# Merged weight words in SBUF instead of PSUM, casts moved to VectorE, one chunk loaded later

## The chip, the cores and the metric

The kernel runs on one core of a Trainium2 chip. A core has TensorE (PE; its weight loads are listed as PEld), VectorE (DVE), ScalarE (ACT), GpSimd (POOL) and SyncE (SP, which only issues transfers and notes here). Each engine works through its own queue in order; semaphores join the queues. The metric is the device time of one launch in microseconds (us); lower is better.

## The reference, cut to what matters

```
w = softmax(weight_gen, axis=-1)               # (4, 4096, 8, 7): 7 taps for each of 8 heads
x_unf = 7 shifted copies of zero-padded x      # x: (4, 4096, 192), 24 channels per head
x2 = einsum('bshk,bskhg->bshg', w, x_unf)      # dynamic causal convolution
h = x2.reshape(16384, 192) @ w_in              # (192, 2048)
g = h            where h >= 1
    0            where h <= -1
    (h + 1)**2/4 elsewhere
out = g @ w_out                                # (2048, 192)
```

All is float32. TensorE multiplies in a shorter format, so the kernel splits every operand into a high and a low part and adds the products that matter.

## The kernel before, in words

The 16384 tokens are cut into 32 blocks of 512. For each block the convolution makes x, a transpose turns it, and it is split into hc (high) and hl (low). The 2048 hidden units are 16 groups of 128, worked on as 8 pairs; with 32 blocks that makes 256 pairs. A pair has a first product (`gemm1_pair`, 18 matmuls into two PSUM banks psh), a gate on ScalarE and VectorE (`relu`, `square`, `act_g`), a split of the gate into gh on ScalarE and gl on VectorE (`split_g`), and, two pairs later, a second product into the banks o (`gemm2_part`, two parts of 16 matmuls).

The weights are not ready when block 0 starts: they are decoded during it, in 8 chunks, chunk c being the w_in columns and w_out rows of pair c. Each chunk has two parts, w_in (part 0) and w_out (part 1). The steps for a chunk are:

- `load_weights(c)`: SyncE fetches the raw words into one of 4 buffers r.
- `cast_act` or `cast_dve`: the upper half of each word is turned into a half-precision head, on ScalarE or VectorE (line 327 or 331). One part is 384 elements wide.
- `merge(c, part)`: VectorE shifts the word and joins it with the head (line 340). It reads r and head, both in SBUF, and writes psw, a bank of the same four PSUM banks (pool `ps_h`) that the first product writes.
- `high(c, part)`: ScalarE copies psw into whi or wo, the high part (line 352).
- `low(c, part)`: VectorE subtracts the high part from psw and writes wlo or the second half of wo (line 356).

`early_pair(w)` handles the gate of pair w and decodes chunk w + 1 in one hand-written order, for w = 2 to 6. `first_pairs` does the same for pairs 0 and 1 with chunks 0 to 2, `edge_pair` ends block 0. Everything is emitted under a manual schedule: the order in the code is the order in each queue.

GpSimd meanwhile computes the convolution of block 1 (`conv`, lines 179 and 189: products of 1.55 us and adds of 1.85 us) in pieces that `wave(count)` takes from a list. Each piece waits for the newest entry of `marks`, that is the last merge or VectorE cast emitted before it. When the 13 pieces are done, ScalarE copies a strip (`again`), TensorE turns the result (`turn1`), and x of block 1 can be split; the first pair of block 1 needs that.

The second part of `gemm2_part` waits for a note: a no-operation on SyncE's queue, behind whatever transfers that queue has still to issue.

Of the kernel before, what the change touches and what calls it, by code (L numbers as in the profile page):

```python
# [10 lines left out]
F32 = mybir.dt.float32  # L11
F32R = mybir.dt.float32r
# [5 lines left out]
ALU = mybir.AluOpType  # L18
# [4 lines left out]
def kernel(  # L23
# [21 lines left out]
    nc = tc.nc  # L45
    P = 128
# [6 lines left out]
    NF = DFF // P  # L53
# [10 lines left out]
    N = n * P  # L64
# [15 lines left out]
    xt = ctx.enter_context(tc.tile_pool(name="xt", bufs=2))  # L80
    up = ctx.enter_context(tc.tile_pool(name="up", bufs=3))
    gp = ctx.enter_context(tc.tile_pool(name="gp", bufs=6))
    op = ctx.enter_context(tc.tile_pool(name="op", bufs=2))
    raw = ctx.enter_context(tc.tile_pool(name="raw", bufs=4))
    dram = ctx.enter_context(tc.tile_pool(name="dram", bufs=2, space=bass.MemoryType.DRAM))
    ps_h = ctx.enter_context(tc.tile_pool(name="ps_h", bufs=4, space=bass.MemoryType.PSUM))
# [129 lines left out]
    def conv_summed(b):  # L216

        g, gi = group_of[b]
        wt, xtile = w_t[g], x_t.pop(b)
        near = ps_o.tile([P, 2, 512], F32, tag="o1", name="near")  # L220
        wn = near[:, 0, 0:n * E].rearrange("p (j h k) -> p j h k", j=n, h=H)
        sums = ps_o.tile([P, 2, 512], F32, tag="o0", name="sums")
        acc = sums.rearrange("p a d -> p (a d)")[:, 0:n * D].rearrange("p (j h g) -> p j h g", j=n, h=H)
        nc.scalar.activation(out=wn, in_=wt[:, gi], func=AF.Copy)

        def times(eng, out, w, k):
            return eng.tensor_tensor(
                out=out, in0=xtile[:, k:k + n, :].rearrange("p j (h g) -> p j h g", h=H),
                in1=w[:, :, :, k:k + 1].to_broadcast([P, n, H, G]), op=ALU.mult)

        def alone(eng, w, k):
            t = whole()
            times(eng, by_head(t), w, k)
            again(t)
            return t

        def add(k):
            t = cv.tile([P, n, H, G], F32, tag="T", name="tap")
            times(nc.vector, t, wn, k)
            out = acc  # L240
            if k == KV - 1:
                own.append(whole())
                out = by_head(own[0])
            nc.vector.tensor_tensor(out=out, in0=acc, in1=t, op=ALU.add)

        own = []
        return alone, wn, wt[:, gi], lambda: times(nc.vector, acc, wn, 1), add, own
# [50 lines left out]
    C1 = NC * P  # L298
    CN = C1 + CF * D
    NCH = NF // CF  # L300
    UNIT = 2.0 ** 8
    raw_t, marks = {}, []

    def load_weights(c, behind=None):
        r = raw.tile([P, 4 * CN + 2], U16, tag="r", name="r")
        for h in range(2):
            f = c * CF + h
            load = nc.sync.dma_start(
                out=r[h * Q:(h + 1) * Q, 1:1 + 4 * C1].rearrange("q (k c) -> q k c", k=NC),
                in_=w_in[:, f * P:(f + 1) * P].rearrange("(k q) c -> q k c", q=Q).bitcast(U16))  # L310
            if behind is not None:
                tc.add_manual_dep(load.ins, behind.ins.name, SYNC, reason="the first block goes first")
                behind = None
        nc.sync.dma_start(
            out=r[:, 1 + 4 * C1:1 + 4 * CN].rearrange("p (f c) -> p f c", f=CF),
            in_=w_out[c * CF * P:(c + 1) * CF * P, :].rearrange("(f p) c -> p f c", p=P).bitcast(U16))
        raw_t[c] = r

    def tops(c, part):

        sl = (slice(0, C1), slice(C1, CN), slice(0, CN))[part]
        top = raw_t[c][:, 2:2 + 4 * CN].rearrange("p (c t) -> p c t", t=4)[:, sl, 2]
        return heads[c % 2][:, sl, 1].bitcast(F16), top.bitcast(BF16)

    def cast_act(c, part):
        o, i = tops(c, part)
        nc.scalar.activation(out=o, in_=i, func=AF.Copy, scale=0.5)

    def cast_dve(c, part):
        o, i = tops(c, part)  # L330
        marks.append(nc.vector.tensor_scalar(out=o, in0=i, scalar1=0.5, scalar2=None, op0=ALU.mult))  # L331

    psw = {}

    def merge(c, part):
        word = raw_t[c].bitcast(U32)[:, 1:1 + 2 * CN].rearrange("p (c t) -> p c t", t=2)[:, :, 0]
        upper = heads[c % 2].rearrange("p c t -> p (c t)").bitcast(U32)
        psw[c, part] = ps_h.tile([P, 512], F32, tag="h", name="psw")
        sl = (slice(0, C1), slice(C1, CN))[part]
        marks.append(nc.vector.scalar_tensor_tensor(  # L340
            out=psw[c, part].bitcast(U32)[:, 0:sl.stop - sl.start], in0=word[:, sl], scalar=13, in1=upper[:, sl],
            op0=ALU.logical_shift_right, op1=ALU.bitwise_or))
# [7 lines left out]
    def high(c, part):  # L350
        hi, lo, src = views(c, part)
        nc.scalar.activation(out=hi, in_=src, func=AF.Copy)  # L352

    def low(c, part):
        hi, lo, src = views(c, part)
        nc.vector.tensor_tensor(out=lo, in0=src, in1=hi.bitcast(F32), op=ALU.subtract)  # L356
        del psw[c, part]
# [27 lines left out]
    def relu(i):  # L385

        u = up.tile([P, 512], F32, tag="u", name="u")
        u_t[i] = u[:, 0:N]
        nc.scalar.activation(out=u_t[i], in_=h_t[i][:, 0:N], func=AF.Relu, scale=0.5 * UNIT, bias=0.5)  # L389

    def square(i):
        nc.scalar.activation(out=u_t[i], in_=u_t[i], func=AF.Square, scale=UNIT ** -0.5)  # L392

    def act_g(i):

        uv, pv = u_t.pop(i), h_t[i][:, 0:N]
        nc.vector.scalar_tensor_tensor(out=pv, in0=uv, scalar=1.0 / UNIT, in1=pv, op0=ALU.min, op1=ALU.max)  # L397

    def split_g(i):
        gv = h_t.pop(i)[:, 0:N]  # L400
        gh = gp.tile([P, 512], F32R, tag="gh", name="gh")
        gl = gp.tile([P, 512], F32R, tag="gl", name="gl")
        nc.scalar.activation(out=gh[:, 0:N], in_=gv, func=AF.Copy)  # L403
        nc.vector.tensor_tensor(out=gl[:, 0:N], in0=gv, in1=gh[:, 0:N].bitcast(F32), op=ALU.subtract)  # L404
        g_t[i] = (gh, gl)

    notes = []
# [89 lines left out]
    for b in range(2, NB):  # L497
        w = (b - 2) * NP
# [34 lines left out]
    with tc.manual_schedule():  # L533
# [19 lines left out]
        alone, near, far, second, add, own = conv_summed(0)  # L553
# [11 lines left out]
        for k, t in enumerate(pieces):  # L565
            for c in range(NC):
                turn_sum(src, t, k == 0, k == len(pieces) - 1, c)
        merge(0, 0)
        cast_dve(0, 1)
        high(0, 0)  # L570
        run(s1[4:6])
        low(0, 0)
        run(split_x(0, src, [nc.vector] * NC))
        cast_dve(1, 2)
        merge(1, 0)
        turned1 = whole()
        n_ops = conv(1, nc.gpsimd, marks, turned1)

        def wave(count):
            for _ in range(min(count, len(n_ops))):  # L580
                n_ops.pop(0)()
# [6 lines left out]

        def first_pairs():
            merge(0, 1)  # L590
            merge(1, 1)
            tc.add_manual_dep(s1[6]().ins, marks[-1].ins.name, SYNC, reason="the decoding of a chunk goes first")
            load_weights(4)
            load_weights(5)
            relu(0)
            high(1, 0)
            low(1, 0)
            gemm1_pair(1)
            cast_act(2, 0)
            high(0, 1)  # L600
            high(1, 1)
            low(0, 1)
            low(1, 1)
            cast_dve(2, 1)
            merge(2, 0)
            merge(2, 1)
            wave(3)
            load_weights(6)
            square(0)
            relu(1)  # L610
            high(2, 0)
            high(2, 1)
            square(1)
            act_g(0)
            low(2, 0)
            low(2, 1)
            act_g(1)
            split_g(0)
            relu(2)
            square(2)  # L620
            split_g(1)
            relu(3)
            square(3)
            act_g(2)
            act_g(3)
            split_g(2)
            split_g(3)
            cast_act(3, 0)
            cast_dve(3, 1)

        def early_pair(w):
            i, j, c = 2 * w, 2 * w + 1, w + 1
            merge(c, 0)
            merge(c, 1)
            wave(1)
            if c + 4 < NCH:
                load_weights(c + 4)
            relu(i)
            high(c, 0)
            high(c, 1)  # L640
            low(c, 0)
            low(c, 1)
            square(i)
            relu(j)
            square(j)
            act_g(i)
            if c + 1 < NCH:
                cast_dve(c + 1, 1)
            wave(1)
            act_g(j)  # L650
            split_g(i)
            split_g(j)
            if c + 1 < NCH:
                cast_act(c + 1, 0)

        def edge_pair(w):
            i, j = 2 * w, 2 * w + 1
# [18 lines left out]
        for w in range(NS // 2 + LAGP):  # L676
            i, j = 2 * w, 2 * w + 1
# [74 lines left out]
```

## Time and profile before

| | us |
|---|---|
| median of 3 runs | 1144.56 (1143.82 to 1144.73) |
| the profiled execution | 1144.88 |
| its span, first to last instruction | 1142.4 |
| TensorE busy | 1128.4 (99%) |
| ScalarE busy | 964.5 (84%) |
| VectorE busy | 834.3 (73%) |
| GpSimd busy | 792.4 (69%) |

Outside the span lie 2.5 us. TensorE's granted clock over the whole span is 0.997 of 2.4 GHz. Block 0 occupies the first 60 us; blocks 1 to 31 fill the rest.

### The profile page before, as it was taken

The numbers are of one execution on the slowest core, as the hardware profiler recorded it, in microseconds if no ns is written. First come the engines' busy times: TensorE is split into PE (matmuls) and PEld (weight loads), VectorE is DVE, ScalarE is ACT, GpSimd is POOL, SyncE is SP. The second block draws the span as 40 slices with busy tenths as digits, with TensorE's granted clock in tenths as the row PEclk, the third lists the DMA queues.
The fourth block names the chain that finished last, engine by engine and source line by source line (L and its number), as shares of the span: only waits on it lengthen the run. The fifth ranks groups of instructions, "written<-read, shape, count | busy, mean of one in ns | idle before, by whom it ended". The sixth has DMA issues, their size and how long they took to land.

```text
span 1142.4 us, 32241 instructions
## 1 busy us (share of the span) xinstructions
PE 1128.4 (99%) x12885; PEld 1112.8 (97%) x12885; DVE 834.3 (73%) x1271; ACT 964.5 (84%) x1745; POOL 792.4 (69%) x511
## 2 busy tenths in 40 slices
PE   7999999999999999999999999999999999999998
PEld 5889999999999999999999999999999999999998
DVE  8887867777676777767777677776767777677765
ACT  6878888888888888888888888888888888888886
POOL 4699876777857678486686866778576785866310
PEclk9899999999999999999999999999999999999999
DMA  9512222222222122222122222222222122221100
GB/s 230 116 67 83 92 85 92 72 64 79 90 78 91 59 74 89 73 96 90 44 90 73 86 91 78 65 73 90 77 92 72 61 91 82 81 91 43 48 24 29
DMA packets 84053, 91.43 MB, mean 80 GB/s; under 512 B 5056, under 2 KB 75712, under 8 KB 83904
## 3 DMA queue, kind: packets, MB, share of 16 engines
q1 hardware_dynamic: 83904, 89.39, 24.6%
q8 instruction: 101, 1.65, 0.6%
q14 instruction: 48, 0.39, 0.1%
HBM read 64.99 MB, written 24.38 MB: 78 GB/s over the span
## 4 chain that ended last, share of the span: by engine, by line
PE 96%; ACT 1%; DVE 1%; DMA 0%; POOL 0%; issue 0%; SPq 0%; DVEq 0%; POOLq 0%
PE psh L378 49%; PE o L432 46%; PE psx L267 1%; DMA x<-in_x_dram 0%; ACT u L392 0%; ACT u L389 0%; ACT gh L403 0%; DVE psh L397 0%; DVE psw L340 0%; ACT whi L352 0%; POOL piece L189 0%; POOL acc L189 0%; ACT wo L352 0%; DVE gl L404 0%; DVE wo L356 0%
## 5 line engine op out<-in xcount | busy, mean ns | idle before, releaser
L432 PE MATMUL o<-wo,gh 64*128 64x384 f32 x4096 | 638.3, 353 | 1.0 <-SPq L441 1.0
L432 PE MATMUL o<-wo,gl 64*128 64x192 f32 x4096 | 615.1, 247 | 0.0
L432 PEld LDWEIGHTS o<-wo,gh 64*128 64x128 f32 x4096 | 609.3, 184 | 2.4 <-SPq L441 1.2
L432 PEld LDWEIGHTS o<-wo,gl 64*128 64x128 f32 x4096 | 591.3, 188 | 0.7
L397 DVE SCALAR_TENSOR_TENSOR psh<-u,psh 128x512 f32<-128x512 f32 x512 | 354.4, 695 | 282.2 <-ACT u L392 281.8
L378 PE MATMUL psh<-hc,whi 64*128 64x512 f32 x1536 | 436.6, 396 | 3.6 <-DVE wlo L356 2.5
L378 PE MATMUL psh<-hc,wlo 64*128 64x512 f32 x1536 | 430.5, 389 | 0.0
L378 PE MATMUL psh<-hl,whi 64*128 64x512 f32 x1536 | 429.5, 388 | 0.0
L389 ACT ACTIVATE u<-psh 128x512 f32<-128x512 f32 x512 | 301.4, 589 | 79.0 <-PE psh L378 77.8
L404 DVE TENSOR_TENSOR gl<-psh,gh 128x512 fp32r<-128x512 f32 x512 | 345.2, 684 | 15.5 <-ACT gh L403 1.1
L403 ACT ACTIVATE gh<-psh 128x512 fp32r<-128x512 f32 x512 | 299.0, 591 | 64.7 <-DVE psh L397 64.7
L189 POOL TENSOR_TENSOR acc<-acc,pr 128x768 f32<-128x768 f32 x185 | 343.4, 1856 | 6.5 <-DVE head L331 2.8
L392 ACT ACTIVATE u<-u 128x512 f32<-128x512 f32 x512 | 324.3, 633 | 16.0
L179 POOL TENSOR_TENSOR pr<-x,w 128x768 f32<-128x768 f32 x186 | 286.6, 1548 | 7.0 <-DVE psw L340 7.0
L378 PEld LDWEIGHTS psh<-hc,whi 64*128 64x128 f32 x1536 | 270.6, 185 | 8.7 <-DVE wlo L356 3.9
L378 PEld LDWEIGHTS psh<-hl,whi 64*128 64x128 f32 x1536 | 270.5, 185 | 3.1 <-DVE hl L259 0.3
L378 PEld LDWEIGHTS psh<-hc,wlo 64*128 64x128 f32 x1536 | 270.9, 186 | 1.6
L259 POOL TENSOR_TENSOR hl<-XT,hc 128x512 fp32r<-128x512 f32 x90 | 115.8, 1303 | 206.9 <-PE o L432 151.6
L179 POOL TENSOR_TENSOR acc<-x,w 128x768 f32<-128x768 f32 x31 | 47.9, 1546 | 70.2 <-DVE w L155 68.3
L258 ACT ACTIVATE hc<-XT 128x512 fp32r<-128x512 f32 x90 | 55.5, 618 | 0.0
L284 DVE STREAM_TRANSPOSE T<-acc 128x768 f32<-128x768 f32 x30 | 50.2, 1672 | 0.0
L457 DVE SCALAR_TENSOR_TENSOR osb<-o,osb 128x384 f32<-128x384 f32 x64 | 32.5, 548 | 2.8 <-ACT osb L456 2.8
(44 smaller groups left out, 188.8 us busy)
## 6 DMA issues: line engine op xcount, KB each, us to landing
x<-in_x_dram SPq DMA_DIRECT2D x28, 960.0 KB, 5.0
XT<-D SPq DMA_DIRECT2D x180, 128.0 KB, 2.7
out_dram<-osb SPq DMA_DIRECT2D x31, 384.0 KB, 3.1
D<-T SPq DMA_DIRECT2D x30, 384.0 KB, 2.3
x<-in_x_dram SPq DMA_DIRECT2D x4, 945.0 KB
w<-in_weight_gen_dram SPq DMA_DIRECT2D x15, 224.0 KB, 2.6
r<-in_moe_w_in_dram SPq DMA_DIRECT2D x16, 192.0 KB, 7.3
r<-in_moe_w_out_dram SPq DMA_DIRECT2D x8, 384.0 KB, 12.5
```

Of the source, the lines that this page charges most:

```text
L179: held(eng.tensor_tensor(out=t, in0=xtile[:, k:k + n, :].rearrange("p j (h g) -> p j h g", h=H), in1=wt[:, gi, :, :, k:k + 1].to_broadcast ...
L189: held(eng.tensor_tensor(out=o, in0=s, in1=t, op=ALU.add))
L258: ops.append(lambda c=c: nc.scalar.activation(out=hc[:, c], in_=src[c], func=AF.Copy))
L259: ops.append(lambda c=c: lows.append(engines[c].tensor_tensor(out=hl[:, c], in0=src[c], in1=hc[:, c].bitcast(F32), op=ALU.subtract)))
L284: lambda: nc.vector.transpose(out=T.rearrange("p b c j -> p b j c"), in_=acc.rearrange("p j (r b) -> p b j r", b=R)),
L378: nc.tensor.matmul(out=pair[h][:, 0:N], lhsT=l[rows, f // 2, (c + h) % NC if b < 2 else c], rhs=r[rows, c], start=(s == 0), stop=(s == len ...
L389: nc.scalar.activation(out=u_t[i], in_=h_t[i][:, 0:N], func=AF.Relu, scale=0.5 * UNIT, bias=0.5)
L392: nc.scalar.activation(out=u_t[i], in_=u_t[i], func=AF.Square, scale=UNIT ** -0.5)
L397: nc.vector.scalar_tensor_tensor(out=pv, in0=uv, scalar=1.0 / UNIT, in1=pv, op0=ALU.min, op1=ALU.max)
L403: nc.scalar.activation(out=gh[:, 0:N], in_=gv, func=AF.Copy)
L404: nc.vector.tensor_tensor(out=gl[:, 0:N], in0=gv, in1=gh[:, 0:N].bitcast(F32), op=ALU.subtract)
L432: mm = nc.tensor.matmul(out=o_t[b][turn][:, k, 0:cols], lhsT=g_t[i][l][rows, t * P:(t + 1) * P], rhs=wo[rows, f].rearrange("p s d -> p (s ...
```

## The change

There are four edits.

1. `merge` writes to one SBUF tile `words` (four slots of 384 columns, taken from the pool that later holds XT) in place of a PSUM bank. `high` and `low` therefore read SBUF.
2. In `early_pair` VectorE casts both parts of the next chunk in one instruction (`cast_dve(c + 1, 2)`, 768 wide), and the ScalarE cast is dropped. This is for chunks 4 to 7.
3. `load_weights(6)` moves from `first_pairs` to the start of `early_pair(2)`.
4. `act_g` and `split_g` test `i in far`; for those units the gate would be written to SBUF and GpSimd would form gl.

```
-    psw = {}
+    psw, words = {}, []
...
-        psw[c, part] = ps_h.tile([P, 512], F32, tag="h", name="psw")
+        if not words:
+            words.append(xt.tile([P, 4, C1], F32, tag="XT", name="words", bufs=1))
+        psw[c, part] = words[0][:, 2 * part + c % 2]
...
+    whole_g = {}
+    far = [2 * w for w in range(1, NF // 2 - 1)]
...
+        to = pv
+        if i in far:
+            whole_g[i] = gp.tile([P, 512], F32R, tag="gl", name="gl")
+            to = whole_g[i][:, 0:N].bitcast(F32)
-        nc.vector.scalar_tensor_tensor(out=pv, in0=uv, scalar=1.0 / UNIT, in1=pv, op0=ALU.min, op1=ALU.max)
+        nc.vector.scalar_tensor_tensor(out=to, in0=uv, scalar=1.0 / UNIT, in1=pv, op0=ALU.min, op1=ALU.max)
...
-        nc.vector.tensor_tensor(out=gl[:, 0:N], in0=gv, in1=gh[:, 0:N].bitcast(F32), op=ALU.subtract)
+        low = nc.gpsimd if i in far else nc.vector
+        low.tensor_tensor(out=gl[:, 0:N], in0=gv, in1=gh[:, 0:N].bitcast(F32), op=ALU.subtract)
...
-            load_weights(6)
...
+            if c == 3:
+                load_weights(6)
...
-                cast_dve(c + 1, 1)
+                cast_dve(c + 1, 2)
...
-            if c + 1 < NCH:
-                cast_act(c + 1, 0)
```

The name `far` is assigned a second time in the same function, in a line that the diff does not touch and that runs before the first `act_g`:

```
alone, near, far, second, add, own = conv_summed(0)
```

From there on `far` is a view of the softmax weights of block 0, not the list of units.

VectorE, one turn of `early_pair` in the kernel before: two merges, two low parts, the gate of one unit (psh<-u), a cast, the gate of the other, two gl.

```order
44 L340 SCALAR_TENSOR_TENSOR psw<-r,head 128x384 x2
45 L356 TENSOR_TENSOR wlo<-psw,whi 128x384
46 L356 TENSOR_TENSOR wo<-psw,wo 128x2x192
47 L397 SCALAR_TENSOR_TENSOR psh<-u,psh 128x512
48 L331 TENSOR_SCALAR head<-r 128x384
49 L397 SCALAR_TENSOR_TENSOR psh<-u,psh 128x512
50 L404 TENSOR_TENSOR gl<-psh,gh 128x512 x2
```

The same turn in the changed kernel:

```order
44 L342 SCALAR_TENSOR_TENSOR words<-r,head 128x384 x2
45 L358 TENSOR_TENSOR wlo<-words,whi 128x384
46 L358 TENSOR_TENSOR wo<-words,wo 128x2x192
47 L406 SCALAR_TENSOR_TENSOR psh<-u,psh 128x512
48 L331 TENSOR_SCALAR head<-r 128x768
49 L406 SCALAR_TENSOR_TENSOR psh<-u,psh 128x512
50 L418 TENSOR_TENSOR gl<-psh,gh 128x512 x2
```

The order is the same; psw has become words, and the cast is twice as wide. Both gl of the pair are still formed by VectorE, and the gate is still written to psh.

ScalarE, from the end of one `early_pair` into the next, before (head is the cast):

```order
42 L403 ACTIVATE gh<-psh 128x512 x2
43 L327 ACTIVATE head<-r 128x384
44 L389 ACTIVATE u<-psh 128x512
45 L352 ACTIVATE whi<-psw 128x384
46 L352 ACTIVATE wo<-psw 128x2x192
47 L392 ACTIVATE u<-u 128x512
48 L389 ACTIVATE u<-psh 128x512
```

And in the changed kernel:

```order
41 L416 ACTIVATE gh<-psh 128x512 x2
42 L391 ACTIVATE u<-psh 128x512
43 L354 ACTIVATE whi<-words 128x384
44 L354 ACTIVATE wo<-words 128x2x192
45 L394 ACTIVATE u<-u 128x512
46 L391 ACTIVATE u<-psh 128x512
```

The cast between two pairs is gone from ScalarE.

GpSimd's queue in the changed kernel, from the softmax step of block 1 through block 1's convolution to the first product of block 2:

```order
14 L155 TENSOR_TENSOR w<-w,s 128x448
15 L179 TENSOR_TENSOR acc<-x,w 128x768
16 L179 TENSOR_TENSOR pr<-x,w 128x768 x3
17 L189 TENSOR_TENSOR acc<-acc,pr 128x768
18 L179 TENSOR_TENSOR pr<-x,w 128x768
...
23 L189 TENSOR_TENSOR acc<-acc,pr 128x768 x2
24 L189 TENSOR_TENSOR piece<-acc,pr 128x4x192
25 L179 TENSOR_TENSOR acc<-x,w 128x768
```

These rows stand in the kernel before with the same operations and the same numbers; nothing moved on this engine, and no gl stands there.

## Rows read from the trace of the kernel before

**Rows 1.** Windows: us, busy us by engine (x instructions), PEclk, DMA share, GB/s
```profile
16.00:30.00 14.00, 9.80 (x82) 7.03 (x80) 13.20 (x26) 11.03 (x23) 6.00 (x5) 0.99 1.09 253
30.00:37.00 7.00, 6.84 (x42) 5.91 (x43) 5.98 (x13) 5.74 (x12) 4.46 (x3) 0.53 1.11 214
37.00:51.00 14.00, 14.00 (x159) 12.73 (x157) 12.90 (x25) 12.11 (x24) 8.65 (x5) 1.00 0.36 110
60.00:150.00 90.00, 90.00 (x1038) 84.79 (x1038) 70.40 (x103) 76.03 (x138) 81.70 (x51) 1.00 0.25 82
```

**Rows 2.** Timeline, VectorE, one turn: start, us, instruction, [idle before]
```profile
44.89 1.02 DVE L340 SCALAR_TENSOR_TENSOR psw<-r,head 128x384 uint32<-128x384 uint32 x2
46.01 0.56 DVE L356 TENSOR_TENSOR wlo<-psw,whi 128x384 fp32r<-128x384 f32 x1
46.48 0.55 DVE L356 TENSOR_TENSOR wo<-psw,wo 128x384 fp32r<-128x384 f32 x1
46.99 0.70 DVE L397 SCALAR_TENSOR_TENSOR psh<-u,psh 128x512 f32<-128x512 f32 x1
47.60 0.38 DVE L331 TENSOR_SCALAR head<-r 128x384 f16<-128x384 bf16 x1
48.14 0.70 DVE L397 SCALAR_TENSOR_TENSOR psh<-u,psh 128x512 f32<-128x512 f32 x1 [0.16 <-ACT u L392]
50.11 0.56 DVE L340 SCALAR_TENSOR_TENSOR psw<-r,head 128x384 uint32<-128x384 uint32 x1
```

**Rows 3.** Timeline, GpSimd, the same turn and the add after it
```profile
46.06 1.55 POOL L179 TENSOR_TENSOR pr<-x,w 128x768 f32<-128x768 f32 x1 [1.33 <-DVE psw L340]
48.06 1.86 POOL L189 TENSOR_TENSOR acc<-acc,pr 128x768 f32<-128x768 f32 x1 [0.45 <-DVE head L331]
51.28 1.83 POOL L189 TENSOR_TENSOR acc<-acc,pr 128x768 f32<-128x768 f32 x1 [1.37 <-ACT whi L352]
```

**Rows 4.** Timeline, VectorE and GpSimd: a softmax step that has both inputs in SBUF
```profile
252.70 0.61 DVE L150 TENSOR_TENSOR w<-w,m 128x448 f32<-128x448 f32 x1
114.56 1.68 DVE L150 TENSOR_TENSOR w<-w,m 128x448 f32<-128x448 f32 x1
114.20 1.56 POOL L179 TENSOR_TENSOR pr<-x,w 128x768 f32<-128x768 f32 x1
115.70 2.25 POOL L189 TENSOR_TENSOR acc<-acc,pr 128x768 f32<-128x768 f32 x1
```

**Rows 5.** Timeline, VectorE and GpSimd, chunks 0 to 2
```profile
18.88 0.55 DVE L356 TENSOR_TENSOR wlo<-psw,whi 128x384 fp32r<-128x384 f32 x1
19.55 1.02 DVE L356 TENSOR_TENSOR wo<-psw,wo 128x384 fp32r<-128x384 f32 x2
22.30 0.54 DVE L356 TENSOR_TENSOR wlo<-psw,whi 128x384 fp32r<-128x384 f32 x1
22.77 0.54 DVE L356 TENSOR_TENSOR wo<-psw,wo 128x384 fp32r<-128x384 f32 x1
24.99 0.69 DVE L404 TENSOR_TENSOR gl<-psh,gh 128x512 fp32r<-128x512 f32 x1 [0.48 <-ACT gh L403]
19.11 0.98 POOL L155 TENSOR_TENSOR w<-w,s 128x448 f32<-128x448 f32 x1 [7.11 <-DVE psw L340]
21.92 1.54 POOL L179 TENSOR_TENSOR acc<-x,w 128x768 f32<-128x768 f32 x1 [1.83 <-DVE psw L340]
```

**Rows 6.** Timeline, VectorE: the low parts of chunks 4 and 5
```profile
35.45 0.56 DVE L356 TENSOR_TENSOR wlo<-psw,whi 128x384 fp32r<-128x384 f32 x1 [0.79 <-ACT whi L352]
40.88 0.56 DVE L356 TENSOR_TENSOR wlo<-psw,whi 128x384 fp32r<-128x384 f32 x1 [0.38 <-ACT whi L352]
```

**Rows 7.** Timeline, VectorE: a cast of both parts
```profile
16.82 0.60 DVE L331 TENSOR_SCALAR head<-r 128x768 f16<-128x768 bf16 x1
```

**Rows 8.** Timeline, TensorE: the second part of the first second product
```profile
27.81 0.45 PE L432 MATMUL o<-wo,gh 64*128 64x384 f32 x2 [1.00 <-SPq L441]
```

**Rows 9.** Page, transfers: issues, KB each, median us from issue to landing
```profile
r<-in_moe_w_out_dram SPq DMA_DIRECT2D x8, 384.0 KB, 12.5
```

More of the change, by code (lines that the diff above doesn't have):

```diff
@@ L392, in square @@
         nc.scalar.activation(out=u_t[i], in_=u_t[i], func=AF.Square, scale=UNIT ** -0.5)
+    whole_g = {}
+    far = [2 * w for w in range(1, NF // 2 - 1)]
     def act_g(i):
         uv, pv = u_t.pop(i), h_t[i][:, 0:N]
-        nc.vector.scalar_tensor_tensor(out=pv, in0=uv, scalar=1.0 / UNIT, in1=pv, op0=ALU.min, op1=ALU.max)
+        to = pv
[3 more added lines that the diff above has]
+        nc.vector.scalar_tensor_tensor(out=to, in0=uv, scalar=1.0 / UNIT, in1=pv, op0=ALU.min, op1=ALU.max)
     def split_g(i):
+        gh = gp.tile([P, 512], F32R, tag="gh", name="gh")
         gv = h_t.pop(i)[:, 0:N]
-        gh = gp.tile([P, 512], F32R, tag="gh", name="gh")
-        gl = gp.tile([P, 512], F32R, tag="gl", name="gl")
+        if i in far:
+            gl = whole_g.pop(i)
+            gv = gl[:, 0:N].bitcast(F32)
+        else:
+            gl = gp.tile([P, 512], F32R, tag="gl", name="gl")
         nc.scalar.activation(out=gh[:, 0:N], in_=gv, func=AF.Copy)
-        nc.vector.tensor_tensor(out=gl[:, 0:N], in0=gv, in1=gh[:, 0:N].bitcast(F32), op=ALU.subtract)
+        low = nc.gpsimd if i in far else nc.vector
+        low.tensor_tensor(out=gl[:, 0:N], in0=gv, in1=gh[:, 0:N].bitcast(F32), op=ALU.subtract)
         g_t[i] = (gh, gl)
```

## The prediction

> **What bounds the kernel now.** I read the windows first [rows 1]. From 60 us on TensorE is busy without a gap (90.00 of the next 90 us), so blocks 1 to 31 are matmul time, and nothing in the change touches them. Only block 0, before 60 us, has anything to win or lose: TensorE is busy 9.80 of 14 us from 16 to 30, and its granted clock is 0.53, that is mostly 1.2 GHz, from 30 to 37. So the question is when block 1's first pair can start; a microsecond there is a microsecond of the total.
>
> The next view is the timeline of VectorE over one turn of `early_pair` [rows 2]. From the merge at 44.89 to the next at 50.11 a turn takes 5.22 us. Blocks 1 to 31 need (1142.4 - 60)/248 = 4.36 us per pair, so in block 0 TensorE waits on the turn, not the reverse. The turn is one chain through two queues: merge, high parts, square, relu and square of the other unit, its gate at 48.14 (the 0.16 before it is the wait for the square), gh, gl, and behind gl in VectorE's queue the next merge. VectorE stands on it twice, so what delays its queue ahead of 48.14 by more than 0.16 lengthens the turn. The end of block 0 hangs on the same chain: GpSimd's last two adds, from 51.28 on, wait for chunk 7's merge [rows 3], and block 1's x is turned after them.
>
> **The change part by part.**
>
> *GpSimd's gl* costs nothing, because it isn't there: `far` names something else by the time it is asked, and the changed kernel's order shows every gl still on VectorE and GpSimd's queue unchanged.
>
> *The later load* frees SyncE's queue, whose note held TensorE for 1.00 us at 27.81 [rows 8]. Its worth is 0: the next first product waits for chunk 3's low part on the turn's chain, so it waits longer by what it arrives sooner. Chunk 6 is cast two turns and a part of one after its new place (the cast is 2.7 into its turn): 2 x 5.22 + 2.7 = 13.1 us at least, more with longer turns. The longest of its transfers took 12.5 us in the middle [rows 9], most of them in the crowded first 37 us. That covers it barely; a late landing would hold VectorE's cast, once, by 1 or 2 us.
>
> *The cast.* ScalarE loses an operation that isn't on the chain; it would only wait longer for the merge. VectorE's cast grows from 0.38 [rows 2] to 0.60 [rows 7], 0.22 against the 0.16 of slack: +0.06 a turn alone, and all of it once VectorE is late.
>
> *The words in SBUF* are the part with a price. `low` used to read one input from PSUM and one from SBUF; now both lie in SBUF. Before, it runs beside GpSimd unhindered: the one at 46.48 takes 0.55 while a product runs from 46.06 to 47.61 [rows 2, 3]. A softmax step shows what two SBUF inputs do [rows 4]. Alone, 448 elements take 0.61. At 114.56 the same step meets a product that ends at 115.76; it takes 1.68 and ends at 116.24, 0.48 after it. The next add, due at 115.70, ends at 117.95, 1.71 after the step, where an undisturbed one takes 1.86 [rows 3]. So the two engines take turns, each for a whole instruction, and the waiting one has about 0.14 of its start behind it. For 384 elements I take 0.48 x 384/448 = 0.41 after GpSimd's end, and for a product behind a low part 1.55 - 0.14 = 1.41.
>
> The Trainium skill, "SBUF — State Buffer", section "SBUF: two separate sides", says that VectorE with two SBUF inputs and a reading GpSimd instruction share one pair of ports under an exclusive lock, held by whoever starts first for its whole instruction. By that rule `low` is held just as the softmax step is, and the sum below stands; were it a split of bandwidth, each meeting would cost tenths. The trace agrees: 1.68 against 0.61.
>
> `wave(1)` releases a GpSimd piece right after the second merge, so it meets the low parts in every turn. In the turn shown, the first low part starts at 46.01 and the product at 46.06:
> - If VectorE is first, it ends at 46.57, the product at 46.57 + 1.41 = 47.98, the second low part at 48.39, where it was 47.03: +1.36.
> - If GpSimd is first, the product ends at 47.61, the first low part at 48.02, the second 0.47 later at 48.49: +1.46.
>
> The gate at 46.99 moves to about 48.35, the cast (0.61 behind it) ends at 49.56, and the second gate starts there, not at 48.14: 1.4 per turn. The bounds are 0.7 (VectorE keeps the ports across its two low parts, below) and 1.5.
>
> Four such turns lead from chunk 3's merge to chunk 7's: 4 x 1.4 = 5.6. Two of them have slack now: the low parts of chunks 4 and 5 waited 0.79 and 0.38 for a high part delayed by TensorE [rows 6], against 0.09 in the turn of rows 2. A slower turn finds TensorE on time; I subtract 0.70 + 0.29, about 1.0. Turns: **+4.6**.
>
> At the start [rows 5] the softmax step on GpSimd at 19.11 asks while the low part of 18.88 runs: it goes from 19.43 to 19.43 + 0.84 = 20.27, and the low part of 19.55 ends at 20.68, not 20.10: **+0.6** for all behind it. Then the three products released at 21.92 follow each other without a gap. The low part of 22.30 waits for the first (23.46) and ends at 23.87; the second takes its turn until 25.28; the low part of 22.77 ends at 25.69, not 23.31: +2.4. Behind it 0.48 was idle, at 24.99, which goes: **+1.9**.
>
> At the end the add of 51.28 may wait for a low part, 0 to 0.4: **+0.2**.
>
> Sum: 4.6 + 0.6 + 1.9 + 0.2 = 7.3. On the profiled execution that is 1144.88 + 7.3 = 1152.2; on the median of the runs, 0.32 lower, 1151.9. I predict **1152.0 us**. The bounds of the meetings give +2.8 to +8.5.
>
> **The rivals.**
>
> *Low parts are not held.* If the step at 114.56 was held by something that `low` lacks, GpSimd costs nothing. Left are 0.06 a turn and a first product that, no longer needing the banks of psw, can start on whi alone, some tenths sooner; the POOL end of the chain allows a few tenths either way: 1144.4. This is the case on the other side. Against it speaks that `low` has the same operation, type and places as the softmax step. It decides at a low part of 0.55 beside a running product.
>
> *VectorE keeps the ports.* Its two low parts follow each other 0.47 apart, before the first has ended. If GpSimd can't get between them, in the turns both finish on time, the product ends at 47.03 + 1.41 = 48.44, and the cast, if it is held as well, ends some 0.47 after, at 48.9, in place of 48.14 for the gate: 0.8 a turn, 3.2 - 1.0 = 2.2; at the start only the first product is waited for, 1.0 - 0.48 = 0.5 more: +2.8, 1147.4. For it speaks that the first low part is 0.05 ahead; against it, that the next add in rows 4 got its turn right behind one step, and that at chunk 2 GpSimd is ahead anyway.
>
> *The clock falls again.* Before, it fell to 0.53 after a stretch with TensorE busy 70% of the time [rows 1], and 7 us at that level lose 0.47 x 7 = 3.3 us of matmuls. With turns of 6.6 us and 4.36 us of work, TensorE is busy 66% until block 0 ends, so another such stretch is near. Inside the turns their gaps of 2.2 us swallow most of it. If it reaches past the end of block 0, it costs about 2.5 more: 1154.5.
>
> **How the numbers follow.** The forecast has 0.56, the falling clock 0.18, the kept ports 0.14, the free low parts 0.12. Within 0.2% (2.3 us, about what a measurement of this kernel can tell from no change) lie most of the free low parts and an edge of the kept ports: 0.11. Faster by over 0.2% is left 0.03, since a turn can't get shorter than its chain. Slower has 0.86. The range runs from just under the kept ports, 1147, to the falling clock and the upper bound of the meetings with a little over, 1156; it leaves out the free low parts and some tails. The likeliest case's own range is 1150 to 1153.5.
>
> **What would show it.** In the profile after, the low parts of chunks 2 to 7 average well over 1 us, where they took 0.55; some reach 1.9. The distance between merges in the last turns is about 6.6 instead of 5.22, TensorE's gaps before the first products of pairs 4 to 7 are 1.5 to 2 us, and block 1's first pair starts near 67. ScalarE's four casts are gone without a trace in the total, and the wait on SyncE at 27.81 is gone too. The prediction is wrong if low parts stay at 0.55 beside running products, or if merges stay 5.2 apart; then the time stays where it was.

## The result and the profile after

The changed kernel takes **1152.91 us** (median of 6 runs, 1151.55 to 1153.42) against 1144.29 us for the kernel before on the same chip (median of 6). The ratio is 1.0067, with a 95% interval of 1.0052 to 1.0082: slower by 8.6 us. The execution profiled took 1151.55 us, with a span of 1149.7; that is the shortest of the six.

The windows of the kernel after come first, with the columns of [rows 1], now cut at the places where block 0 ends.

```profile
30.00:37.00 7.00, 3.87 (x26) 2.89 (x26) 6.80 (x12) 4.76 (x9) 2.87 (x2) 0.85 0.83 183
37.00:51.00 14.00, 12.18 (x134) 10.72 (x130) 13.60 (x21) 9.24 (x18) 8.06 (x5) 0.95 0.36 103
51.00:60.00 9.00, 6.68 (x58) 5.24 (x60) 8.68 (x12) 6.77 (x13) 5.70 (x3) 0.93 0.10 27
60.00:67.00 7.00, 6.47 (x54) 4.80 (x52) 5.99 (x10) 5.64 (x12) 6.92 (x6) 0.84 0.00 0
67.00:75.00 8.00, 8.00 (x94) 7.27 (x94) 6.12 (x10) 5.86 (x12) 8.00 (x5) 1.00 0.26 92
```

TensorE is busy for 3.87 of the 7 us from 30 on, where it was busy for 6.84; it is full only from 67 us, not from 60. VectorE is busy for 6.80 of 7 and 13.60 of 14 (an instruction that is held counts as busy): the turn is now VectorE's. The next view groups VectorE's instructions of the stretch from 16 to 62 us (busy us and mean ns behind the bar).

```profile
L358 DVE TENSOR_TENSOR wo<-words,wo 128x384 fp32r<-128x384 f32 x8 | 11.9, 1492 | 0.2 <-ACT wo L354 0.2
L342 DVE SCALAR_TENSOR_TENSOR words<-r,head 128x384 uint32<-128x384 uint32 x15 | 7.6, 550 | 0.0
L358 DVE TENSOR_TENSOR wlo<-words,whi 128x384 fp32r<-128x384 f32 x7 | 6.3, 895 | 0.6
```

The low parts (line 358) stand at 1492 and 895 ns in the mean; the undisturbed ones in [rows 2] took 0.55 us. The merges, with an SBUF output now, stay at 550. Why the low parts are longer is seen where VectorE's and GpSimd's timelines of one turn stand together (start, us, instruction, idle before):

```profile
43.90 1.02 DVE L342 SCALAR_TENSOR_TENSOR words<-r,head 128x384 uint32<-128x384 uint32 x2
45.04 0.56 DVE L358 TENSOR_TENSOR wlo<-words,whi 128x384 fp32r<-128x384 f32 x1
45.51 1.90 DVE L358 TENSOR_TENSOR wo<-words,wo 128x384 fp32r<-128x384 f32 x1
47.34 0.68 DVE L406 SCALAR_TENSOR_TENSOR psh<-u,psh 128x512 f32<-128x512 f32 x1
47.93 0.61 DVE L331 TENSOR_SCALAR head<-r 128x768 f16<-128x768 bf16 x1
48.42 0.71 DVE L406 SCALAR_TENSOR_TENSOR psh<-u,psh 128x512 f32<-128x512 f32 x1
50.41 1.01 DVE L342 SCALAR_TENSOR_TENSOR words<-r,head 128x384 uint32<-128x384 uint32 x2
45.06 1.94 POOL L179 TENSOR_TENSOR pr<-x,w 128x768 f32<-128x768 f32 x1 [1.09 <-DVE words L342]
48.62 1.84 POOL L189 TENSOR_TENSOR acc<-acc,pr 128x768 f32<-128x768 f32 x1 [1.63 <-DVE head L331]
```

The first low part asks 0.02 ahead of the product and takes 0.56. The product takes 1.94 in place of 1.55 [rows 3]: it ran behind the low part. The second low part asks at 45.51, gets its turn behind the product's end at 47.00, and ends at 47.41, 0.41 after it. From merge to merge it is 50.41 - 43.90 = 6.51, where it was 5.22 [rows 2].

At the start of block 0 the same thing happens with three products in a row, and the note on SyncE no longer holds TensorE (VectorE, GpSimd, then TensorE):

```profile
22.80 1.57 DVE L358 TENSOR_TENSOR wlo<-words,whi 128x384 fp32r<-128x384 f32 x1
24.29 1.89 DVE L358 TENSOR_TENSOR wo<-words,wo 128x384 fp32r<-128x384 f32 x1
22.41 1.54 POOL L179 TENSOR_TENSOR acc<-x,w 128x768 f32<-128x768 f32 x1 [2.23 <-DVE words L342]
23.91 3.68 POOL L179 TENSOR_TENSOR pr<-x,w 128x768 f32<-128x768 f32 x2
27.82 0.46 PE L446 MATMUL o<-wo,gh 64*128 64x384 f32 x2
```

Chunk 2's low parts took 0.54 each in [rows 5]. The wait of 1.00 at 27.81 [rows 8] is gone, and nothing came of it: TensorE's next first product, at 32.05, waits longer instead. This kernel alone doesn't show that the later load removed the wait: with the words in SBUF alone and the load at its old place it is gone as well, since TensorE comes there later. The first kernel below, with the words in PSUM and the later load, does: no wait there, and the next first product waits 2.21 us, where it waited 0.94 before.

### The profile page after: what moved, and what is told of

Same layout as the page of the kernel before. It is cut to its first block, busy times and chain, and to the rows that moved or that the text cites. A ratio compares the mean times of both kernels' runs of the same rounds, so it can differ in the third digit from the quotient of the medians.

```text
span 1149.7 us, 32226 instructions
## 1 busy us (share of the span) xinstructions
PE 1130.6 (98%) x12885; PEld 1113.7 (97%) x12885; DVE 844.3 (73%) x1271; ACT 963.6 (84%) x1741; POOL 795.0 (69%) x511
## 4 chain that ended last, share of the span: by engine, by line
PE 95%; DVE 3%; ACT 1%; issue 1%; DMA 0%; SPq 0%; DVEq 0%
PE psh L380 48%; PE o L446 46%; DVE psh L406 1%; PE psx L267 1%; DVE wo L358 1%; DMA x<-in_x_dram 0%; ACT gh L416 0%; DVE wlo L358 0%; DVE gl L418 0%; DVE words L342 0%; ACT whi L354 0%; DVE head L331 0%; DVE piece L227 0%; ACT u L391 0%; SPq L135 0%
## 5 line engine op out<-in xcount | busy, mean ns | idle before, releaser
L380 PE MATMUL psh<-hc,whi 64*128 64x512 f32 x1536 | 430.9, 397 | 7.5 <-ACT whi L354 7.5
L380 PEld LDWEIGHTS psh<-hc,whi 64*128 64x128 f32 x1536 | 266.8, 185 | 11.4 <-ACT whi L354 9.3
L380 PEld LDWEIGHTS psh<-hc,wlo 64*128 64x128 f32 x1536 | 267.5, 186 | 7.3 <-DVE wlo L358 5.4
L380 PEld LDWEIGHTS psh<-hl,whi 64*128 64x128 f32 x1536 | 266.8, 185 | 2.5 <-DVE hl L259 0.3
```

Source lines behind the costliest of these rows:

```text
L380: nc.tensor.matmul(out=pair[h][:, 0:N], lhsT=l[rows, f // 2, (c + h) % NC if b < 2 else c], rhs=r[rows, c], start=(s == 0), stop=(s == len ...
```

## The experiments

Each kernel was timed beside the kernel before on one chip. The table sets two places of each profiled execution against each other: chunk 7's merge, which is the last of block 0, and how long after it block 1's first pair starts. The ratios are to the kernel before in the same round; its median there was 1143.81 (words in PSUM again to w_in alone), 1143.89 (w_out alone to GpSimd's gl) and 1143.93 (after again, and the filled ones), a little below the 1144.29 of the first row.

| Kernel | chunk 7's merge, us | from there to block 1's first product | profiled run | median of runs | ratio to before, 95% interval |
|---|---|---|---|---|---|
| before | 50.11 | 9.71 | 1144.88 | 1144.29 | |
| after | 56.91 | 10.30 | 1151.55 | 1152.91 | 1.0067, 1.0052 to 1.0082 |
| after, again | 57.01 | 11.66 | 1152.79 | 1152.79 | 1.0074, 1.0062 to 1.0086 |
| words in PSUM again | 50.65 | 9.70 | 1144.69 | 1143.56 | 0.9998, 0.9989 to 1.0006 |
| words in SBUF alone | 56.01 | 11.66 | 1151.82 | 1150.78 | 1.0063, 1.0051 to 1.0075 |
| no pieces in the turns | 51.93 | 11.66 | 1147.81 | 1147.33 | 1.0036, 1.0020 to 1.0052 |
| w_in alone in SBUF | 52.12 | 10.09 | 1147.30 | 1147.52 | 1.0035, 1.0024 to 1.0046 |
| w_out alone in SBUF | 53.43 | 9.88 | 1148.39 | 1148.33 | 1.0034, 1.0022 to 1.0045 |
| piece behind the low part | 55.39 | 11.76 | 1151.55 | 1151.50 | 1.0054, 1.0035 to 1.0074 |
| products later at chunk 2 | 55.14 | 11.66 | 1151.34 | 1150.15 | 1.0048, 1.0032 to 1.0064 |
| GpSimd's gl, words in PSUM | 52.75 | 10.79 | 1148.67 | 1149.10 | 1.0040, 1.0028 to 1.0051 |
| after, gaps filled | 56.77 | 11.65 | 1153.28 | 1153.21 | 1.0083, 1.0066 to 1.0100 |
| PSUM, gaps filled | 49.91 | 9.71 | 1144.86 | 1144.65 | 1.0009, 1.0001 to 1.0018 |

**The words in PSUM again**, with the cast, the later load and the order of the kernel after:

```diff
-        if not words:
-            words.append(xt.tile([P, 4, C1], F32, tag="XT", name="words", bufs=1))
-        psw[c, part] = words[0][:, 2 * part + c % 2]
+        psw[c, part] = ps_h.tile([P, 512], F32, tag="h", name="psw")
```

> The kernel after with the merged words back in PSUM; the whole-chunk cast, the later load and the moved instructions stay. My theory (low parts held because both inputs lie in SBUF beside GpSimd's two-input pieces): everything that was lost comes back. Low parts of chunks 2 to 7 take 0.55 us again, merges of the last turns lie 5.2 to 5.3 us apart (5.22 before, at most 0.06 more for the larger cast), total 1144.3, at most 1144.8. Rival 'the cast of 768 instead of 384 costs, or ScalarE without its casts, or the later load': the turns stay at 6.5 and the total near 1152.

All of the loss comes back: 1143.56 against 1143.81 for the kernel before in that round, with turns of 5.23 and one of 5.42. A low part beside a running product (VectorE, GpSimd):

```profile
41.30 0.56 DVE L356 TENSOR_TENSOR wlo<-psw,whi 128x384 fp32r<-128x384 f32 x1
41.78 0.55 DVE L356 TENSOR_TENSOR wo<-psw,wo 128x384 fp32r<-128x384 f32 x1
41.36 1.54 POOL L179 TENSOR_TENSOR pr<-x,w 128x768 f32<-128x768 f32 x1 [1.11 <-DVE psw L340]
```

With one input in PSUM, neither engine is longer than alone. The cast, the load and the moved instructions cost nothing that these runs can tell.

**The words in SBUF, and nothing else**: the kernel before with the same three lines put in.

> The kernel before with the merged words in SBUF and nothing else of the change. My theory: nearly the whole loss. Low parts wait as in the kernel after (0.5 to 0.6 for the one that is first, 1.9 for the one behind a product); the cast of 384 is 0.22 shorter than that of 768, so a turn is about 6.3 in place of 6.5; 4 x 1.07 less the slack of 1.0, and 0.5 at the start, 2.0 at chunk 2, 0.6 at the end: about +6.4, total 1150.7 (1150 to 1151.5). Rival 'another part of the change carries it': turns of 5.2, total 1144.3. If both share it, something between, near 1148.

1150.78, as expected (1150.7), with turns of 6.28 to 6.30. The second low part of a turn is held as in the kernel after:

```profile
45.05 1.90 DVE L358 TENSOR_TENSOR wo<-words,wo 128x384 fp32r<-128x384 f32 x1
```

So the place of the words carries the loss, from both sides: 7.0 us of 8.6 by itself. The wider cast accounts for 0.9 of the rest: a turn is 6.51 with it, and the last merge stands at 56.91 instead of 56.01. That price exists only beside words in SBUF, when VectorE is late; with the words in PSUM the same cast cost nothing that the runs above can tell.

**No pieces in the turns**: the kernel after with

```diff
+        n_ops = [n_ops[0], n_ops[1], n_ops[9], n_ops[12]]
...
-            wave(1)
+            wave(1 if w == NP - 2 else 0)
...
-            wave(1)
             act_g(j)
```

> The kernel after without GpSimd's pieces of block 1's convolution beside the turns: of its products only those released at chunk 2 stay (the three), and the last add; the others are left out, so block 1's convolution is incomplete. My theory (the pieces hold the low parts): inside the turns every low part takes 0.55, merges are 5.2 to 5.3 apart, and what stays is the start (0.5) and chunk 2 (2.0): total about 1146.5 (1145.5 to 1147), block 1's first pair about 2 to 2.5 us later than before. Rival 'reading the words from SBUF is slow in itself': the second low part still takes 1.9, turns stay at 6.5, total 1152.

VectorE in a turn:

```profile
41.42 1.02 DVE L342 SCALAR_TENSOR_TENSOR words<-r,head 128x384 uint32<-128x384 uint32 x2
42.56 0.56 DVE L358 TENSOR_TENSOR wlo<-words,whi 128x384 fp32r<-128x384 f32 x1
43.04 0.55 DVE L358 TENSOR_TENSOR wo<-words,wo 128x384 fp32r<-128x384 f32 x1
```

Reading the words from SBUF is not slow in itself: without a product the low parts take 0.56 and 0.55, and the turns 5.25. What stays is the start, 30.92 for chunk 3's merge as in the kernel after (30.89). The total, 1147.33, is 0.3 above the expected range, and its runs lie far apart (1144.31 to 1155.57), so this verdict rests on the trace; the 11.66 in the table has a cause of its own, below.

**One half of the words in SBUF**: w_in alone, and w_out alone (`part == 1` in place of `part == 0`).

```diff
+        if part == 0:
             if not words:
...
+        else:
+            psw[c, part] = ps_h.tile([P, 512], F32, tag="h", name="psw")
```

> The kernel after with only the first half of each chunk's words (w_in) in SBUF, the second half (w_out) in PSUM. My theory (the instruction that starts first keeps the pair of ports, the other waits for its end): in a turn the first low part starts some 0.02 to 0.05 us ahead of the product, so it takes 0.55, the product takes 1.9, and the second low part is not held because one of its inputs is in PSUM: turns of 5.2 to 5.4, total 1145 to 1146.5 (a few tenths at the start, about 1 at chunk 2, where the product is ahead). In a turn where the product is ahead the first low part takes 1.9 and that turn is 1.4 longer. Rival 'each low part with its words in SBUF is slow by itself': half the loss, first low parts of 1.2 to 1.9 in every turn, total about 1148. Rival 'VectorE and GpSimd share the bandwidth': first low parts near 1, turns of 5.7, total near 1147.

> The kernel after with only the second half of each chunk's words (w_out) in SBUF and the first half (w_in) in PSUM: the mirror of the kernel with w_in alone in SBUF. My theory (whole instructions take turns, and whoever starts first decides): the first low part never waits and holds nothing up, the product runs its 1.55 beside it, and the second low part, due 0.47 later, waits for the product's end plus about 0.4: it takes 1.4 to 1.5 in every turn (not in some, as the first half did), turns are 6.2 to 6.3 (5.23 + 1.0), and the total is 4 x 1.0 - 1.0 of slack, and 0.3 to 0.9 at the start and chunk 2: +3.3 to +4, near 1147.5. Rival 'a split of the bandwidth': low parts near 0.8 to 1.0 and products near 2.0, turns of 5.5, near 1145.5.

With w_in alone (VectorE, then GpSimd, in two turns):

```profile
29.26 1.92 DVE L361 TENSOR_TENSOR wlo<-words,whi 128x384 fp32r<-128x384 f32 x1
42.35 0.56 DVE L361 TENSOR_TENSOR wlo<-words,whi 128x384 fp32r<-128x384 f32 x1
42.83 0.55 DVE L361 TENSOR_TENSOR wo<-psw,wo 128x384 fp32r<-128x384 f32 x1
43.91 0.89 DVE L331 TENSOR_SCALAR head<-r 128x768 f16<-128x768 bf16 x1
29.23 1.54 POOL L179 TENSOR_TENSOR pr<-x,w 128x768 f32<-128x768 f32 x1 [1.87 <-DVE psw L345]
42.38 1.93 POOL L179 TENSOR_TENSOR pr<-x,w 128x768 f32<-128x768 f32 x1 [1.10 <-DVE psw L345]
```

At 29.23 the product is 0.03 ahead, and the low part takes 1.92; at 42.35 the low part is 0.03 ahead, and it takes 0.56 and the product 1.93. So 0.03 us decide which of the two loses about 1.4 us. The product was ahead in the turns of chunks 3 and 4 (6.50 and 6.59 long), the low part in the others. Those came out at 5.45, 0.2 more than a free turn, because the later product now holds the cast: 0.89, ended 0.49 after the product. The total of 1147.52 is 1 us above the expected range, with two turns lost where I had counted on none or one.

With w_out alone the second low part is held in every turn: it takes 1.45 to 1.51 (0.55 alone), and the product runs its 1.54 unhindered. The turns are 6.04 to 6.12.

```profile
42.81 1.51 DVE L361 TENSOR_TENSOR wo<-words,wo 128x384 fp32r<-128x384 f32 x1
42.36 1.54 POOL L179 TENSOR_TENSOR pr<-x,w 128x768 f32<-128x768 f32 x1 [1.09 <-DVE words L345]
```

The profiled execution is 3.5 above that of the kernel before, as expected (+3.3 to +4); the median, 1148.33, is 0.8 above the expected 1147.5. A split of bandwidth would have lengthened both engines' instructions; in neither kernel does it.

**The piece behind the low part**: released by the second low part, not by the second merge.

```diff
             merge(c, 1)
-            wave(1)
...
             low(c, 1)
+            wave(1)
             square(i)
```

> The kernel after, but in each turn GpSimd's first piece is released by the second low part, not by the second merge. My theory: both low parts take 0.55 again, but the piece then meets the cast of 768, and the runs so far show a cast that ends 0.49 after a product (0.88 instead of 0.60), so a cast is held as well: it ends about 0.9 later than it would, turns are near 6.1, and with the start and chunk 2 as in the kernel after the total is about 1149.5: moving the piece saves some 0.4 a turn, not 1.3. Rival 'only instructions with two inputs in SBUF are held': casts stay at 0.60, turns 5.25, total near 1146.5.

```profile
44.14 0.56 DVE L358 TENSOR_TENSOR wlo<-words,whi 128x384 fp32r<-128x384 f32 x1
44.61 0.56 DVE L358 TENSOR_TENSOR wo<-words,wo 128x384 fp32r<-128x384 f32 x1
45.13 0.70 DVE L406 SCALAR_TENSOR_TENSOR psh<-u,psh 128x512 f32<-128x512 f32 x1
45.73 1.60 DVE L331 TENSOR_SCALAR head<-r 128x768 f16<-128x768 bf16 x1
45.31 1.55 POOL L179 TENSOR_TENSOR pr<-x,w 128x768 f32<-128x768 f32 x1 [2.24 <-DVE wo L358]
```

Both low parts are free, and the cast takes 1.60 in place of 0.61, from 0.42 behind the product's start to 0.47 behind its end. The gate at 45.13, with one input in PSUM, runs its 0.70 beside the product. The turns are 6.13 to 6.20, as my theory had it (6.1). The wait was moved, not removed. The total is 2 us above the 1149.5 expected; in the profiled execution that is the 11.76 of the table against 9.8. The Trainium skill, "SBUF — State Buffer", section "SBUF: two separate sides", counts among the instructions that take the shared ports those of VectorE in a two-port mode, beside those with two SBUF inputs; the cast's 1.60 agrees. That this cast runs in such a mode is concluded from its wait alone.

**The products later at chunk 2**: `wave(3)` moved behind chunk 2's second low part, and released by it.

> The kernel after, but GpSimd's first three products wait for chunk 2's second low part instead of its second merge. My theory (the 1.96 lost at chunk 2 are two products that each came between): chunk 2's low parts take 0.55, chunk 3's merge is about 1.9 earlier than in the kernel after (29.0 instead of 30.9), the turns stay at 6.5, total about 1.9 below the kernel after: near 1150.5 (1150 to 1151.5). Rival: what is won at chunk 2 is given back, because the later products run into the next instructions of VectorE with two inputs in SBUF (the cast and merges of chunk 3) and hold them: then chunk 3's merge moves by under 1 us and the total by under 1.

Chunk 3's merge is at 29.04 (expected 29.0; 30.89 after), chunk 2's low parts take 0.55 each, and the turns stay at 6.50 to 6.58. The total is 6.3 above the kernel before, where the kernel after is 8.6 and 8.9 above it: 2.3 to 2.6 less, where 1.9 was expected. The term of chunk 2 is shown.

**GpSimd's gl**: the words in PSUM, and the list of units under a name that nothing else takes. The gate goes to a tile in SBUF.

```diff
-    far = [2 * w for w in range(1, NF // 2 - 1)]
+    far_units = [2 * w for w in range(1, NF // 2 - 1)]
...
-        low = nc.gpsimd if i in far else nc.vector
+        low = nc.gpsimd if i in far_units else nc.vector
```

> The kernel after with its words back in PSUM (whose total is that of the kernel before), and with the list of units under a name of its own, so that GpSimd really forms the low part of the even gate of pairs 1 to 6; the gate then goes to an SBUF tile. My theory: GpSimd's low part stands behind the turn's add, starts when that ends, and runs beside the next turn's merges, whose two inputs lie in SBUF: the first merge waits for its end. It lasts about 1.25 (1.85 x 512/768), the merge is due some 0.2 after its start, so about 1 us a turn is lost, 4 to 5 turns less the slack of 1.0: +3 to +4, near 1147.3; merges of 1.2 to 1.6 instead of 0.55. Rival 'off the path': VectorE is relieved of 0.7 a turn, the turn stays 5.2 by its chain or falls to 5.0, total 1143 to 1144.

```profile
46.39 2.12 DVE L340 SCALAR_TENSOR_TENSOR psw<-r,head 128x384 uint32<-128x384 uint32 x2
44.60 1.84 POOL L189 TENSOR_TENSOR acc<-acc,pr 128x768 f32<-128x768 f32 x1 [0.75 <-DVE head L331]
46.41 1.68 POOL L416 TENSOR_TENSOR gl<-wide,gh 128x512 fp32r<-128x512 f32 x1
```

The two merges, 1.02 us together before, take 2.12: GpSimd's low part stands between them. So the second merge is held, not the first, as I had expected. The last three turns are 6.3 to 6.4, +1.1; the first is 5.24. In the profiled execution that makes 2.64 at the last merge and 1.08 behind it, since that merge is held as well (10.79 in the table): +3.8, as expected (+3 to +4). The medians are further apart, by 5.2: that round's median of the kernel before lies 1.0 below its profiled execution, and the median here 0.4 above the profiled one. So with the words in PSUM a low part on GpSimd makes the kernel slower. What it would do beside words in SBUF, as the change meant it, was not run.

**The kernel after once more**, for the second column of the table.

> The kernel after, unchanged, profiled once more beside new runs. In the traces so far the distance from chunk 7's merge to the first product of block 1's first pair is 9.7 to 9.9 us where the granted clock stays at 1.00 after that merge, 10.3 in the kernel after (a stretch of 3.4 us at 0.5 lies mostly inside a gap of TensorE) and 11.7 where such a stretch lies wholly behind the merge. Theory: the runs of the kernel after come in levels 1.4 us apart by where that stretch falls; an execution at the upper level (about 1153) shows it behind 60 us and a distance of 11.7, one at the lower (1151.5) shows 10.3. Rival: the upper level comes from somewhere past block 0; then the distance is 10.3 at either level.

The windows of this execution and of the first one, behind the last merge (columns as in [rows 1]); first the new one:

```profile
56.00:64.00 8.00, 4.32 (x36) 2.86 (x34) 7.11 (x10) 5.98 (x12) 6.81 (x5) 1.00 0.01 2
64.00:67.30 3.30, 3.30 (x21) 2.82 (x20) 2.48 (x4) 2.07 (x5) 3.30 (x3) 0.50 0.00 0
67.30:75.00 7.70, 7.70 (x86) 6.83 (x86) 5.75 (x9) 5.41 (x10) 7.70 (x5) 0.99 0.09 23
```

```profile
56.00:64.00 8.00, 5.88 (x36) 3.81 (x32) 7.01 (x10) 6.00 (x13) 6.81 (x5) 0.79 0.00 0
64.00:67.30 3.30, 3.24 (x38) 2.84 (x40) 3.08 (x5) 3.07 (x7) 3.30 (x3) 1.00 0.00 0
```

In the new one TensorE does 21 matmuls from 64.0 to 67.3, at a granted clock of 0.50 (1.2 GHz); in the first execution it does 38, at 1.00. TensorE's timeline of the new one, with the wait before block 1's x is turned, and with the first product of block 1's first pair:

```profile
62.94 1.16 PE L267 MATMUL psx<-ident,piece 128*128 128x128 f32 x8 [2.07 <-DVE gl L418]
68.67 0.41 PE L380 MATMUL psh<-hc,whi 64*128 64x512 f32 x2
```

The wait ends with a gl of VectorE; GpSimd's last add had ended at 62.50. Behind it TensorE has no gap to the first product, so every matmul at 0.50 moves it. In the first execution the clock fell at 58.8 and was back at 62.2, ahead of the turning at 62.82, so the slower matmuls only filled this wait (0.47 instead of 2.07) and cost nothing. The new one's block 1 starts 11.66 after the last merge, not 10.30: 1.36, and the profiled times differ by 1.24. This execution is as the theory had it. All executions with 11.65 to 11.76 in the table have a stretch of 0.50 behind the start of that turning, those with 9.7 to 10.8 have none there. In the former TensorE had waited 2.04 to 2.24 us just before the turning, in the latter 0.43 to 1.45; no run tests whether that matters. For the runs without a trace I infer the levels from the spacing alone: four of the first six runs lie at 1152.86 to 1153.42, two at 1151.55 and 1151.57. The five new ones, 1150.84 to 1154.23, don't fall into two such levels, so more than this stretch varies.

**The gaps filled**, in the kernel after and in the one with the words in PSUM:

```diff
             pair = [ps_h.tile([P, 512], F32, tag="h", name="psh") for _ in range(2)]
+            drive({2: 3, 3: 5, 4: 3, 5: 5, 6: 5, 7: 5}.get(w, 0), pair[0])
```

> The kernel after with extra matmuls (an identity on itself, 0.22 us each) ahead of the first product of pairs 2 to 7, 3 to 5 of them, which fill TensorE's gaps there and are overwritten by the product. Theory: the gaps are only waiting time, so the turns stay at 6.5, but the clock no longer falls in block 0, or at least not behind the last merge: the distance from the last merge to block 1's first pair is 9.7 to 9.9 and every run lies near 1151.0, with a spread under 1 us, 1.5 to 2 below the median of the kernel after. Rival 'the clock has no part in it': the same time and the same spread as the kernel after.

> The kernel with the words back in PSUM (cast and load as after) with such extra matmuls in TensorE's two long gaps ahead of pairs 2 and 3, 3 and 7 of them: a version meant to beat both kernels. Theory: the stretch of half clock from 32 to 36 us goes, chunk 4's low part no longer waits 0.37 for its high part, and a later turn is 0.19 shorter: 0.4 us less than with the words in PSUM alone, near 1143.3. Rival: the extra matmuls come late and push the products behind them: up to 1 us more. Rival: no difference that can be measured.

Neither gained time. The gaps ahead of pairs 5 to 7 shrank to 0.20 to 0.35, but the clock fell all the same, behind the gap at the end of pair 7, which I had not filled (TensorE; columns as in the timelines):

```profile
56.32 1.25 PE L208 MATMUL psh<-ident 128*128 128x512 bf16 x5
57.93 0.50 PE L381 MATMUL psh<-hc,whi 64*128 64x512 f32 x2 [0.35 <-ACT whi L354]
62.70 1.79 PE L267 MATMUL psx<-ident,piece 128*128 128x128 f32 x8 [2.06 <-DVE gl L419]
```

The runs lie at 1149.98 to 1158.62, wider than without. In the second kernel the clock stayed at 1.00 from 18 us on, yet the median is 1144.65, not 1143.3. Chunk 7's merge came 0.74 sooner than with the words in PSUM alone, but that is no gain of the filling: the merges ahead of every added matmul already started 0.87 sooner (17.71 against 18.58). The turn of chunk 4 did become 0.19 shorter (5.42 to 5.23), but that of chunk 3 grew from 5.23 to 5.54, as the first rival had it: the seven matmuls ahead of pair 3 start at 30.42, only after the wait of 1.93 that they were to fill, and the product follows them at 32.02. Why the median lies 0.7 above that round's kernel before stays open. No version here beats the kernel before.

## Why the prediction was right, and where it wasn't

- **The mechanism** was right: low parts with both inputs in SBUF and GpSimd's pieces go one at a time. PSUM again takes the loss away, SBUF alone brings it, leaving out the pieces frees the low parts, and each half is held by the rule that I took from one softmax step [rows 4].
- **The start**, forecast +0.6: chunk 2's merge went from 20.76 to 21.27, +0.5.
- **Chunk 2**, forecast +1.9: chunk 3's merge is 2.47 later, 1.96 more.
- **The turns**, forecast +4.6: four turns took 21.69 before and 26.02 after, +4.33. Per turn it is 1.29, not 1.4: I put the larger cast in with its whole 0.61, but the next gate starts 0.49 after it. The slack to subtract was 21.69 - 4 x 5.22 = 0.81, not 1.0. The two errors partly cancel.
- **The tail**, forecast +0.2: +0.59 in the profiled execution. The last two adds take 2.22 and 2.02, where they took 1.83 and 1.85: each stands behind a low part, where I had allowed for one of them, and 0 to 0.4. The path itself I had only half right: before, the turning of block 1's x waits for the last add; in the kernel after it waits for a gl of VectorE, which comes after chunk 7's held low part (2.19). Before, then after:

```profile
53.19 1.85 POOL L189 TENSOR_TENSOR piece<-acc,pr 128x768 f32<-128x768 f32 x1
55.10 1.09 PE L267 MATMUL psx<-ident,piece 128*128 128x128 f32 x8 [0.44 <-POOL piece L189]
```

```profile
60.38 2.02 POOL L189 TENSOR_TENSOR piece<-acc,pr 128x768 f32<-128x768 f32 x1
62.82 1.17 PE L267 MATMUL psx<-ident,piece 128*128 128x128 f32 x8 [0.47 <-DVE gl L418]
```

  From the last merge the turning starts 5.91 behind, not 4.99, and 0.33 of this comes back later, as a wait of TensorE behind the turning, 0.52 at 58.02 in the kernel before, is gone. Without the pieces the last add ends at 55.33 and the turning still starts only at 57.86, behind a gl, 5.93 after the last merge.
- **The falling clock**, which I gave 0.18 as a rival, isn't a rival but an addition that comes in some executions. Inside the turns it costs next to nothing, as I wrote: the repeated execution ran at 0.50 from about 33 to 40 and its last merge is 0.10 later. Behind the start of the turning it costs 1.36 against the first execution, where I put about 2.5 on the sum.
- **The total** therefore came out right with some luck. My sum on the profiled execution was 1152.2; that execution took 1151.55. The four terms measure 0.51 + 1.96 + 4.33 + 0.59 = 7.4 (forecast 7.3), and the span grew by 7.3; the time grew by 6.7 only, because what lies outside the span fell from 2.5 to 1.85, for which I had no term. The median lies 1.4 above that execution, by the clock if the other runs are like the repeated one, and the clock was no part of the sum. The rest of the difference between the medians (8.6) and the profiled executions (6.7) is that the profiled execution of before was 0.6 above its median.
- **The parts costed at nothing** were nothing: ScalarE's casts, the later load (chunk 6's cast never waits), and GpSimd's gl, which isn't there.
- **The signs** held but for one: TensorE's gaps before the first products of pairs 4 to 7, forecast at 1.5 to 2 us, are 1.53 and 1.55 at pairs 6 and 7, but 0.76 at pair 5 and none at pair 4. At pair 4 TensorE comes late, after a wait of 1.45 in the middle of pair 3's product, for the held low part; at pair 5 the stretch at 0.50 from 34.9 us on took up time (with the words in SBUF alone, and no such stretch there, it is 1.34).
- **The rivals**: low parts that are not held falls with every trace in which a piece meets low parts with their words in SBUF. VectorE keeping the ports falls with 45.51, where the product got in between two low parts 0.47 apart.

## What to carry to other kernels

Before an operand is moved from PSUM to SBUF, count the SBUF inputs of the instruction that reads it: with two of them, it and GpSimd's work alternate, and an instruction on the chain that waits for a piece costs most of that piece (1.29 a turn here, for pieces of 1.55). Add up per turn all that goes through those ports on both engines (here 3.4 us of pieces, 1.0 of merges, 1.0 of low parts and 0.5 of cast make 5.9, in a turn of 5.2; with the words in PSUM it is 4.9): where the sum is above the turn, a piece that is moved may take the wait along, as the one that was tried did. It is a rule of thumb: with w_out alone the sum is 5.4, and the turn is 6.1. Where a profiled execution and the median differ, look at the granted clock in the stretch between the chain's end and the first stage that TensorE bounds.

## What the hardware showed that I had not expected

- A cast with one input (bf16 to f16) is held behind a product too: 1.60 in place of 0.61, while a gate with one input in PSUM beside the same product keeps its 0.70.
- Who is first decides at 0.02 to 0.03 us, and differs from turn to turn in one kernel.
- GpSimd slips between two VectorE instructions that start 0.47 apart; what waits has some 0.15 of its start behind it (a held product takes 1.94 from its request, and the low part ahead of it ended 0.54 after that request: 1.40 in place of 1.55).
- The granted clock's stretches at 0.50 come at other places in two executions of one kernel (24.6, 34.9 and 58.8 us; 33.2 and 64.0). What sets them stays open. With most gaps filled, one execution shows none from 29 to 62 us and then one behind the gap left open; with w_out alone and nothing filled, one execution shows none from 18 to 72 us. So these runs don't tell whether filling steers them.
